# A fused attention and feed-forward kernel on one core: a step more in layer 2's feature chain, later outputs, new pacing of weights and rows

## The chip, the cores and the metric

The kernel runs on one core of one Trainium2 chip. The time is device microseconds of one launch; it was 992.25 us before the change (median of 3 runs, 991.57 to 992.88). The engines are TensorE (PE; its weight loads are PEld), VectorE (DVE), ScalarE (ACT), GpSimd (POOL) and SyncE (SP, which issues nearly all transfers). Each works through its own queue in order.

## The reference

```python
q_p, k_p = phi(q * scale), phi(k * scale)      # phi: exp(h - max h) / sqrt(m), h = x @ omega.T - |x|^2 / 2
kv, z = einsum('bhsm,bhsd->bhmd', k_p, v), sum(k_p, axis=2)
x = (q_p @ kv) / (q_p @ z + 1e-6)              # 4 batches, 8 heads, 576 rows, 64 columns; 128 features
x = x as 2304 x 512
# layer 1: d_ff 1536
xn = x / sqrt(mean(x * x) + 1e-6) * rms_g
x = (silu(xn @ w_gate) * (xn @ w_val)) @ w_out
# layer 2: d_ff 2048
h = x @ w_in
out = (h * cos(h)) @ w_out2                    # 2304 x 512
```

All inputs and the output are float32. The matrix products of the two layers are made of values split in a high and a low part, with three matmuls (high x high, low x high, high x low) in place of one.

## The kernel before

The 2304 tokens are cut in six blocks of 384, and these in three pairs. After attention, layer 1 runs over three groups of features; its second and third group (g = 1 and 2) and all of layer 2 use Strassen-like products: a pair of blocks and a pair of 128-feature tiles take seven products in place of eight. For these the rows of a pair are combined beforehand into T1 to T4 (`mix`, L1111, for layer 2; stored in DRAM and brought back by `bring`, L931).

Layer 2 is a sequence of 24 *periods* (`periods`, L1165): each has one pair of blocks (p) and one pair of feature tiles (fq). In the loop at L1349 a period k issues seven products with `hidden(k, i)`, L1176 (six matmuls of 384 columns each), and behind each product `share[i]` matmuls of the second product of an earlier period (`out2`, L1229, taken one at a time from `stream`; 36 a period, of 512 columns). Period 0's products are woven into the end of layer 1, and what is left of `out2` runs after the loop. Period 1 takes 26 output matmuls, all others 36; so the outputs are 10 matmuls behind a full period.

The products of a period alternate between two PSUM banks, X and Y. ScalarE copies the products 0, 2, 3 and 6 into SBUF (L1190), VectorE adds the others to these (L1193). The next product on a bank needs the copy or the addition before it.

A list of due work sets the order of everything else. `unit()` (L1012 shows in the profile for work issued by it) is called twice a product, so a period has 14 steps; `at(d, f)` puts f into the queues d steps later. A step also advances the preparation of weights by `tempo` (two rates, in parts of a step each).

`cosine` (L1204) turns two rows of h into features in this way: step 1 the phase as an integer (ScalarE), step 2 the two-part reduction (VectorE, L1214 and L1215), step 3 the sine (ScalarE), step 4 the multiplication by h (VectorE, L1225), steps 5 and 6 the split into high (ScalarE, L1046) and low (VectorE, L1049).

Weights come as chunks. A *front* (L187) undoes the packing of a raw chunk: VectorE at L190, L195 and L204, ScalarE at L182 for the next chunk, GpSimd at L209; it asks the raw chunk after next (L170), must wait until the next one's load was asked 9 steps ago (`LAG_OF_RAW`), and the result goes to DRAM (`kept`). A *back* brings chunks in again, combines and splits them (VectorE L274 to L291, ScalarE L214, GpSimd L217); it needs two fronts more than its own chunk, and room in a ring of 20 buffers, which `freed_by` (L1340) opens. Of 56 chunks beyond the first, `FRONTS_BY_2` wants 39 done before layer 2. Within it the rate of fronts is

```python
tempo[:] = 0.0 if loading or k < 4 else wts.rate(len(wts.todo) + 1, 14 * (14 - k)), 0.5 if loading else 1.3
```

where `loading` marks the last period of a run on one pair (k = 2, 5, 11, 14, 19, 21, 23), and `rate(chunks, steps)` spreads the fronts up to that chunk over so many steps.

In layer 1's groups 1 and 2, output rows y go to DRAM and are asked back (`ask`, L1091) some steps (`later`, L1302) after a product of the second half of a session, so that `add_y` (L1099) can add the next sums to them.

Of the kernel before, what the change touches and what calls it, by code (L numbers as in the profile page):

```python
# [38 lines left out]
AF = mybir.ActivationFunctionType  # L39
ALU = mybir.AluOpType  # L40
# [16 lines left out]
def attention_then_ffn(ctx: ExitStack, tc: tile.TileContext, qT, kT, v, omT, wc1, rms_g, wc2, out, B, H, S, D):  # L57
    nc = tc.nc
# [54 lines left out]
    def f32(ap):  # L113
        return ap.bitcast(F32)
# [3 lines left out]
    quarter = const.tile([P, 1], F32, name="quarter")  # L118
    half_pi = const.tile([P, 1], F32, name="half_pi")
# [7 lines left out]
    class Weights:  # L127
# [91 lines left out]
        def split(self, src, key):  # L219
            t = self.buffer()  # L220
            self.high(src, t, slice(0, 512))
            yield
            self.low(src, t, slice(0, 512))
            layer, f, e = key
            if self.paired(layer, f, e) == 0:
                self.out[layer, f, "A11"], self.out[layer, f, "A12"] = (t, 0), (t, 256)
            else:
                self.out[key] = t
            yield
# [172 lines left out]
    wts = Weights()  # L402
# [142 lines left out]
    with tc.manual_schedule():  # L545
# [59 lines left out]
        def job(n):  # L605
            for _ in range(n):
                if len(combined) < limit[0] and jobs and next(jobs[0][1], DONE) is DONE:
                    combined.add(jobs.pop(0)[0])
# [135 lines left out]
        for s, (nm, t) in tiles.items():  # L744
# [4 lines left out]
            else:  # L749
                for i in range(1, 8):  # L750
                    at = s + i + (s >= SLOTS - 1 or i > 1)
# [111 lines left out]
        def silu(blk, f, ps):  # L863
            a = row(F32, f"gv{blk}_{f}")
            nc.scalar.activation(a, ps, AF.Silu)
            return a
# [10 lines left out]
        def out1(g, blk, f, t, first, last, es):  # L877

            if first and es[0] == 0:
                yacc[blk] = [bank_of_sums(f"y_ps{g}_{blk}_{f}_{e}")[:, :NB] for e in range(KD)]  # L880
            w = wts.get(1, f, 2)
            for i, j in ((0, 0), (1, 0), (0, 1)):
                for e in es:
                    nc.tensor.matmul(yacc[blk][e], w[:, i, e * P:(e + 1) * P], t[:, j],  # L884
                                     start=first and i + j == 0, stop=last and j == 1)
            if not last:
                return
            for e in es:
                waits.append((put_away, blk, e, yacc[blk][e]))
# [26 lines left out]
        def halves(name):  # L916
            n = made["t"] % (OWN + EXTRA)
            made["t"] += 1
            if n < OWN:
                return fp.tile([P, 2, NB], F32R, tag="t", name=name, bufs=OWN)  # L920
            return more[0].tile([P, 2, NB], F32R, tag="t", name=name, bufs=EXTRA)

        def two_rows(dt, name):
            return more[0].tile([P, 2, NB], dt, tag="f", name=name, bufs=4)
# [23 lines left out]
        for n, (g, blk, f, first, last) in enumerate(steps):  # L948
# [13 lines left out]
            a = silu(blk, f, ps)  # L962
# [40 lines left out]
        tempo = [0.0, 0.0]  # L1003

        def at(d, f, *args):
            due.setdefault(clock[0] + d, []).append((f, args))

        def unit():
            now = due.setdefault(clock[0], [])
            while now:  # L1010
                f, args = now.pop(0)
                f(*args)  # L1012
            del due[clock[0]]
            flush(1)
            wts.now += 1
            wts.pace(*tempo)
            job(2 if clock[0] % 5 < 2 else 1)
            clock[0] += 1
# [147 lines left out]
        NPER = len(periods)  # L1166
        ends_run = [k + 1 == NPER or periods[k + 1][2] != periods[k][2] for k in range(NPER)]
        begins_run = [k == 0 or ends_run[k - 1] for k in range(NPER)]
# [35 lines left out]
        def cosine(k, h, of, begin=1):  # L1204

            name = "_".join(f"{x}_{f}_{blk}" for x, f, blk in of)
            span = slice(0, 2) if len(of) == 2 else slice(begin, begin + 1)
            h = h[:, span]
            a = two_rows(I32, f"turns{name}")[:, span]
            b = f32(halves(f"r{name}"))[:, span]  # L1210
            r = f32(a)

            def reduce():
                nc.vector.scalar_tensor_tensor(b, a, -TWO_PI_HI, h, op0=ALU.mult, op1=ALU.add)  # L1214
                nc.vector.scalar_tensor_tensor(r, a, -TWO_PI_LO, b, op0=ALU.mult, op1=ALU.add)  # L1215

            def cut(i):
                o = turned[of[i]] = halves("o%d_%d_%d" % of[i])
                split(o, r[:, i])
                at(int(of[i][0] + 1 < NPER), lower, o, r[:, i], nc.vector)  # L1220

            at(1, nc.scalar.activation, a, h, AF.Identity, quarter, 1.0 / (2 * math.pi))
            at(2, reduce)
            at(3, nc.scalar.activation, r, r, AF.Sin, half_pi)
            at(4, lambda: nc.vector.tensor_tensor(r, h, r, op=ALU.mult))  # L1225
            for i in range(len(of)):
                at(5 + i, cut, i)

        def out2(k):  # L1229

# [57 lines left out]
        for k, (g, p) in enumerate(pairs):  # L1288
            fs = list(GROUPS1[g])
            start = base + (g - 1) * PER_GROUP  # L1290
            last_of_group = k + 1 == len(pairs) or pairs[k + 1][0] != g
            nxt = pairs[k + 1] if k + 1 < len(pairs) else (3, sessions[0][1])
            left = UNITS * (len(pairs) - 1 - k) - (30 if k == 0 else 0)
            if k == NPAIR:
                while jobs:
                    job(1)
                combine.close()
                wider.append(extra.enter_context(tc.tile_pool(name="rows", bufs=1, reuse_waits="tile")))
                made["y"] = 0
            front[0] = wts.rate(FRONTS_BY_2, left) if left > 0 else 0.0  # L1300
            tt = {}
            later = 3 if g == 1 else 9  # L1302

            def after_first(i, f):
                if k == 0 and i == 0 and f == fs[1]:
                    out1(*steps[-1][:3], hid.pop(N1 - 1), *steps[-1][3:], range(KD))
                    wts.freed = C1 * G

            def after_second(i, f):
                if f == fs[3]:  # L1310
                    if nxt[0] == 3 or nxt[1] != p:
                        at(2, bring, *nxt, NAMES[i])
                    if i < KD:
                        at(later, ask, g, 2 * p, i)
                    elif i < 7:
                        at(later, ask, g, 2 * p + 1, i - KD)

            duo(g, p, fs[:2], w_bank, tt, after_first)
            if last_of_group:
                wts.freed = start + PER_PAIR  # L1320
            duo(g, p, fs[2:], bank_of_sums, tt, after_second)
            if last_of_group:
                wts.freed = start + 2 * PER_PAIR
            ys(g, p, 0, fs, tt, w_bank)
            at(6, ask, g, 2 * p + 1, 3)
            weave = None
            if k + 1 == len(pairs):
                weave = [lambda i=i: (hidden(0, i), unit()) for i in range(7)]
            ys(g, p, 1, fs, tt, bank_of_sums, weave)
            if last_of_group:  # L1330
                wts.freed = start + PER_GROUP
            if g == 2:
                for m, (name, kk) in enumerate((name, kk) for kk in range(2) for name in ("T1", "T3", "T2", "T4")):
                    at(6 + 3 * m // 2 if p else 6 + (0, 2, 3, 6)[m % 4] + 14 * kk, mix, p, name, kk)

        def stream():
            for k in range(NPER):
                yield from out2(k)

        def freed_by(k):  # L1340
# [4 lines left out]
            elif sessions[n - 1][0] != g and fq == GROUPS2[g][0]:  # L1345
                wts.freed = first_tile[g]

        o = stream()
        for k in range(1, NPER):  # L1349
            loading = ends_run[k]  # L1350
            tempo[:] = 0.0 if loading or k < 4 else wts.rate(len(wts.todo) + 1, 14 * (14 - k)), 0.5 if loading else 1.3
            if ends_run[k - 1]:
                ask_sums(k - 1)
            share = [2, 3, 3, 4, 4, 5, 5] if k == 1 else [5, 5, 3, 5, 6, 6, 6] if begins_run[k - 1] else [5, 5, 5, 5, 5, 5, 6]
            for i in range(7):
                if (k, i) == (len(GROUPS2[0]), 4):
                    assert not whole
                    wider.pop()
                    extra.close()
                    outs.append(ctx.enter_context(tc.tile_pool(name="outs", bufs=1, reuse_waits="tile")))  # L1360
                hidden(k, i)
                unit()
                for _ in range(share[i]):
                    next(o)
                unit()
                if i == 1 and k > 1:
                    freed_by(k - 1)
                if (i, k + 1) == (3, NPER):
                    ask_sums(k)
# [53 lines left out]
```

## Time and profile before

| what | value |
|---|---|
| median of 3 runs | 992.25 us |
| profiled execution | 990.3 us |
| its span | 988.5 us |
| TensorE busy | 957.0 us, 97% |
| VectorE busy | 730.0 us, 74% |
| ScalarE busy | 532.0 us, 54% |
| GpSimd busy | 412.1 us, 42% |
| granted TensorE clock | 0.998 of full |

Busy times are unions of instruction times of one profiled execution. Shares are means over stages that differ, so stretches are looked at by themselves below. In rows of the trace, an instruction's row has its start and duration in us, and in brackets how long its engine stood idle before it and what ended that.

### The profile page before, as it was taken

The numbers are of one execution on the slowest core, as the hardware profiler recorded it, in microseconds if no ns is written. First come the engines' busy times: TensorE is split into PE (matmuls) and PEld (weight loads), VectorE is DVE, ScalarE is ACT, GpSimd is POOL, SyncE is SP. The second block draws the span as 40 slices with busy tenths as digits, with TensorE's granted clock in tenths as the row PEclk, the third lists the DMA queues.
The fourth block names the chain that finished last, engine by engine and source line by source line (L and its number), as shares of the span: only waits on it lengthen the run. The fifth ranks groups of instructions, "written<-read, shape, count | busy, mean of one in ns | idle before, by whom it ended". The sixth has DMA issues, their size and how long they took to land.

```text
span 988.5 us, 16243 instructions
## 1 busy us (share of the span) xinstructions
PE 957.0 (97%) x5761; PEld 895.3 (91%) x5761; DVE 730.0 (74%) x1175; ACT 532.0 (54%) x1143; POOL 412.1 (42%) x377
## 2 busy tenths in 40 slices
PE   9999999998999999999999997999988999999998
PEld 8998999998999999999999996989867879898987
DVE  6787678898854785576786659887898897776766
ACT  7787676676434442535353636554554645464443
POOL 3143348648926875455664743211334121040000
PEclk9999999999999999999999999999999999999999
DMA  8555268876796988766979793857533848306564
GB/s 310 156 175 173 85 226 281 275 286 213 268 334 235 393 279 319 246 191 216 345 270 389 255 343 103 308 187 239 181 127 113 282 139 300 115 22 225 203 253 150
DMA packets 96082, 227.65 MB, mean 230 GB/s; under 512 B 9728, under 2 KB 45184, under 8 KB 96000
## 3 DMA queue, kind: packets, MB, share of 16 engines
q1 hardware_dynamic: 94560, 221.81, 64.8%
q10 hardware_dynamic: 1440, 4.78, 1.4%
q8 instruction: 46, 0.75, 0.3%
q14 instruction: 36, 0.29, 0.1%
HBM read 156.04 MB, written 70.52 MB: 229 GB/s over the span
## 4 chain that ended last, share of the span: by engine, by line
PE 61%; DVE 13%; DMA 8%; issue 6%; POOL 5%; ACT 5%; SPq 1%; ACTq 0%; DVEq 0%; POOLq 0%
PE o_ps L1242 14%; PE Xh L1038 7%; PE gv_ps L831 6%; PE X L1038 6%; PE Yh L1038 5%; PE Y L1038 4%; PE kv_ps L587 4%; PE y L1144 4%; PE y_ps L884 3%; DMA y<-y_dram 3%; PE num_ps L464 2%; PE kp_ps L426 2%; DMA T<-T_dram 1%; DVE r L1214 1%; PE qp_ps L426 1%
## 5 line engine op out<-in xcount | busy, mean ns | idle before, releaser
L1242 PE MATMUL o_ps<-w,o 128*128 128x512 f32 x864 | 225.7, 393 | 1.0 <-DVE o L1274 0.8
L209 POOL TENSOR_TENSOR f<-f,raw 128x512 f32<-128x512 f32 x68 | 94.5, 1390 | 225.2 <-DVE raw L204 193.3
L217 POOL TENSOR_TENSOR w<-b,w 128x512 fp32r<-128x512 f32 x88 | 116.1, 1325 | 169.7 <-ACT w L214 147.0
L1242 PEld LDWEIGHTS o_ps<-w,o 128*128 128x128 f32 x864 | 159.6, 188 | 25.7 <-DVE o L1274 1.1
L831 PE MATMUL gv_ps<-xhl,w 128*128 128x384 f32 x576 | 109.8, 339 | 1.5 <-DVE eT L454 1.3
L1144 PE MATMUL y<-t,w 128*128 128x384 f32 x576 | 102.7, 335 | 1.8 <-POOL w L217 1.8
L831 PEld LDWEIGHTS gv_ps<-xhl,w 128*128 128x128 f32 x576 | 101.8, 190 | 2.6 <-DVE eT L454 2.0
L1144 PEld LDWEIGHTS y<-t,w 128*128 128x128 f32 x576 | 99.9, 188 | 2.8 <-POOL w L217 2.8
L1038 PE MATMUL Xh<-T,w 128*128 128x384 f32 x432 | 88.9, 340 | 5.3 <-ACT h L1190 5.3
L1038 PEld LDWEIGHTS Xh<-T,w 128*128 128x128 f32 x432 | 77.8, 188 | 13.6 <-ACT h L1190 8.2
L1012 ACT ACTIVATE turns<-turns,half_pi 128x768 f32<-128x768 f32 (+1 forms) x50 | 45.6, 913 | 76.7 <-DVE turns L1215 76.7
L1038 PE MATMUL X<-T,w 128*128 128x384 f32 x432 | 81.1, 335 | 0.5 <-POOL w L217 0.3
L1038 PEld LDWEIGHTS X<-T,w 128*128 128x128 f32 x432 | 75.3, 188 | 1.1 <-POOL w L217 0.7
L1012 ACT ACTIVATE turns<-h,quarter 128x768 int32<-128x768 f32 (+1 forms) x50 | 45.6, 912 | 56.6 <-DVE h L1193 56.5
L1225 DVE TENSOR_TENSOR turns<-h,turns 128x768 f32<-128x768 f32 (+1 forms) x50 | 50.6, 1012 | 31.3 <-ACT turns L1012 31.1
L214 ACT CAST w<-b 128x512 fp32r<-128x512 f32 x88 | 50.7, 581 | 30.7 <-DVE b L274 28.2
L1049 DVE TENSOR_TENSOR o<-turns,o 128x384 fp32r<-128x384 f32 x96 | 64.8, 704 | 2.5 <-ACT o L1046 1.3
L1038 PE MATMUL Yh<-B,w 128*128 128x384 f32 x288 | 59.3, 340 | 7.1 <-ACT h L1190 5.7
L1214 DVE SCALAR_TENSOR_TENSOR r<-turns,h 128x768 f32<-128x768 int32 (+1 forms) x50 | 50.2, 1004 | 21.2 <-ACT turns L1012 20.8
L1038 PEld LDWEIGHTS Yh<-B,w 128*128 128x128 f32 x288 | 51.7, 188 | 13.0 <-ACT h L1190 8.0
L884 PE MATMUL y_ps<-t,w 128*128 128x384 f32 x288 | 60.7, 346 | 0.0
L1046 ACT CAST o<-turns 128x384 fp32r<-128x384 f32 x96 | 45.8, 512 | 25.5 <-DVE turns L1225 24.4
(118 smaller groups left out, 1863.9 us busy)
## 6 DMA issues: line engine op xcount, KB each, us to landing
T<-T_dram SPq DMA_DIRECT2D x48, 768.0 KB, 7.0
raw<-wc SPq DMA_DIRECT2D x59, 512.0 KB, 5.0
B<-yh_dram SPq DMA_DIRECT2D x21, 768.0 KB, 5.3
kept<-f SPq DMA_DIRECT2D x56, 256.0 KB, 5.1
b<-kept SPq DMA_DIRECT2D x56, 256.0 KB, 4.6
B<-x_dram SPq DMA_DIRECT2D x15, 768.0 KB, 6.4
x_dram<-xhl SPq DMA_DIRECT2D x12, 768.0 KB, 5.8
s<-x_dram SPq DMA_DIRECT2D x24, 384.0 KB, 6.1
```

What stands on the lines that cost most here:

```text
L209: nc.gpsimd.tensor_tensor(f32(f), f32(f), rest, op=ALU.add)
L214: nc.scalar.copy(t[:, 0, to], src)
L217: nc.gpsimd.tensor_tensor(t[:, 1, to], src, f32(t[:, 0, to]), op=ALU.subtract)
L831: nc.tensor.matmul(o, w[i], x[j], start=n == 0, stop=n == len(terms) - 1)
L884: nc.tensor.matmul(yacc[blk][e], w[:, i, e * P:(e + 1) * P], t[:, j], start=first and i + j == 0, stop=last and j == 1)
L1012: f(*args)
L1038: nc.tensor.matmul(o, w[:, i, c + kk * P:c + (kk + 1) * P], x[:, j, kk], start=begin and n == 0, stop=n == 5, skip_group_check=True)
L1049: engine.tensor_tensor(t[:, 1], a, f32(t[:, 0]), op=ALU.subtract)
L1144: nc.tensor.matmul(acc[e], w[:, i, e * P:(e + 1) * P], t[:, j], start=f == fs[0] and i + j == 0, stop=f == fs[-1] and j == 1)
L1214: nc.vector.scalar_tensor_tensor(b, a, -TWO_PI_HI, h, op0=ALU.mult, op1=ALU.add)
L1225: at(4, lambda: nc.vector.tensor_tensor(r, h, r, op=ALU.mult))
L1242: nc.tensor.matmul(oacc[blk][j], o[:, x, js], w[:, y], start=first and n == 0, stop=last and n == 2)
```

## The change

The chain in `cosine` gets one step more between phase and reduction and one more between reduction and sine, in all periods but the last. Period 1 issues 21 output matmuls in place of 26, so outputs are 15 behind. Rooms in the ring of weights are opened at product 2 in place of product 1. The rate of fronts follows a table of goals per period. The asks of y rows in group 2 come 7 steps after their product in place of 9, and the eight combinations of the pairs 2 and 1 are spread over 8 steps in place of 10.

```diff
@@ cosine
-            at(1, nc.scalar.activation, a, h, AF.Identity, quarter, 1.0 / (2 * math.pi))
-            at(2, reduce)
-            at(3, nc.scalar.activation, r, r, AF.Sin, half_pi)
-            at(4, lambda: nc.vector.tensor_tensor(r, h, r, op=ALU.mult))
+            ph, re, si, mu, cu = (1, 2, 3, 4, 5) if k + 1 == NPER else (1, 3, 5, 6, 7)
+            at(ph, nc.scalar.activation, a, h, AF.Identity, quarter, 1.0 / (2 * math.pi))
+            at(re, reduce)
+            at(si, nc.scalar.activation, r, r, AF.Sin, half_pi)
+            at(mu, lambda: nc.vector.tensor_tensor(r, h, r, op=ALU.mult))
             for i in range(len(of)):
-                at(5 + i, cut, i)
+                at(cu + i, cut, i)
@@ layer 1, groups 1 and 2
-            later = 3 if g == 1 else 9
+            later = 3 if g == 1 else 7
...
-                    at(6 + 3 * m // 2 if p else 6 + (0, 2, 3, 6)[m % 4] + 14 * kk, mix, p, name, kk)
+                    at(6 + 5 * m // 4 if p else 6 + (0, 2, 3, 6)[m % 4] + 14 * kk, mix, p, name, kk)
@@ layer 2
+        FRONT_GOALS = {3: 42, 4: 45, 6: 47, 7: 48, 8: 49, 9: 50, 12: 52, 13: 54, 15: 56, 16: 57}
...
-            tempo[:] = 0.0 if loading or k < 4 else wts.rate(len(wts.todo) + 1, 14 * (14 - k)), 0.5 if loading else 1.3
+            tempo[:] = wts.rate(wts.fused + FRONT_GOALS[k], 14) if k in FRONT_GOALS else 0.0, 0.5 if loading else 1.3
...
-            share = [2, 3, 3, 4, 4, 5, 5] if k == 1 else [5, 5, 3, 5, 6, 6, 6] if begins_run[k - 1] else [5, 5, 5, 5, 5, 5, 6]
+            share = [1, 2, 3, 3, 4, 4, 4] if k == 1 else [5, 5, 3, 5, 6, 6, 6] if begins_run[k - 1] else [5, 5, 5, 5, 5, 5, 6]
...
-                if i == 1 and k > 1:
+                if i == 2 and k > 1:
                     freed_by(k - 1)
```

## Rows read from the trace of the kernel before

**Rows 1.** Busy time by stretch: periods k = 1, 2, 3, 4, 8, 9, 10, 11, 13, 16.
```profile
core 0: us, PE busy (x) PEld busy (x) DVE busy (x) ACT busy (x) POOL busy (x), PEclk, DMA share, GB/s
...
593.43:610.58 17.15, 14.43 (x69) 11.66 (x68) 15.50 (x27) 11.10 (x22) 5.28 (x3) 1.00 0.21 77
610.58:628.92 18.34, 16.11 (x80) 14.20 (x80) 17.67 (x24) 10.58 (x20) 6.84 (x7) 1.00 0.80 287
628.92:644.67 15.75, 15.75 (x79) 14.19 (x78) 12.75 (x16) 7.08 (x12) 3.95 (x3) 1.00 0.56 221
644.67:660.39 15.72, 15.72 (x79) 14.15 (x78) 13.51 (x23) 9.39 (x16) 1.31 (x1) 1.00 0.57 200
...
707.62:725.99 18.37, 16.45 (x79) 13.84 (x77) 16.20 (x20) 9.26 (x18) 7.26 (x5) 1.00 0.39 127
725.99:746.08 20.09, 16.54 (x79) 13.93 (x79) 18.62 (x23) 10.01 (x19) 8.98 (x7) 1.00 0.42 128
746.08:765.96 19.88, 16.80 (x79) 13.84 (x79) 17.11 (x24) 10.49 (x19) 8.90 (x7) 1.00 0.38 111
765.96:782.30 16.34, 16.11 (x79) 14.20 (x80) 13.29 (x16) 10.00 (x17) 4.46 (x4) 1.00 0.87 302
...
798.05:816.84 18.79, 16.62 (x80) 13.89 (x79) 17.91 (x30) 10.22 (x18) 6.04 (x4) 1.00 0.41 140
...
848.34:864.06 15.72, 15.72 (x79) 14.15 (x78) 13.29 (x20) 7.73 (x14) 1.14 (x1) 1.00 0.51 168
```

**Rows 2.** TensorE's instructions in order of time, four that it had to wait for.
```profile
512.96 2.35 PE L1038 MATMUL Y<-T,w 128*128 128x384 f32 x12 [1.54 <-DVE r L1069]
...
581.79 1.31 PE L1038 MATMUL Yh<-B,w 128*128 128x384 f32 x6 [1.43 <-DVE y L1099]
...
740.62 1.31 PE L1038 MATMUL Yh<-B,w 128*128 128x384 f32 x6 [2.43 <-ACT h L1190]
...
804.52 0.98 PE L1242 MATMUL o_ps<-w,o 128*128 128x512 f32 x3 [0.82 <-DVE o L1274]
```

**Rows 3.** ScalarE's instructions in order of time, ahead of the stall at 740.62.
```profile
739.27 0.94 ACT L1012 ACTIVATE turns<-turns,half_pi 128x768 f32<-128x768 f32 x1 [3.21 <-DVE turns L1215]
740.11 0.46 ACT L1190 COPY h<-Yh 128x384 f32<-128x384 f32 x1
```

**Rows 4.** Who waited for whom, whole run: total us, times, longest.
```profile
ACT turns L1012 <- DVE turns L1215: 76.7, 49, 3.9
```

**Rows 5.** VectorE's instructions in order of time, of the first product and of k = 9.
```profile
581.17 0.56 DVE L1099 TENSOR_TENSOR y<-y,y 128x384 f32<-128x384 f32 x1 [1.82 <-DMA y<-y_dram]
...
727.01 1.30 DVE L1214 SCALAR_TENSOR_TENSOR r<-turns,h 128x768 f32<-128x768 int32 x1 [0.74 <-ACT turns L1012]
...
736.20 2.04 DVE L1214 SCALAR_TENSOR_TENSOR r<-turns,h 128x768 f32<-128x768 int32 x1
...
740.23 0.96 DVE L1225 TENSOR_TENSOR turns<-h,turns 128x768 f32<-128x768 f32 x1 [0.66 <-ACT turns L1012]
...
745.14 0.41 DVE L190 TENSOR_SCALAR f<-W 128x512 int32<-128x512 int32 x1
```

**Rows 6.** GpSimd's instructions in order of time, beside L1214 at 736.20.
```profile
736.13 1.29 POOL L217 TENSOR_TENSOR w<-b,w 128x512 fp32r<-128x512 f32 x1 [0.27 <-ACT w L214]
```

**Rows 7.** Groups by line, 630 to 990 us: count, busy us, mean ns, idle before.
```profile
L1242 PE MATMUL o_ps<-w,o 128*128 128x512 f32 x802 | 209.1, 393 | 1.0 <-DVE o L1274 0.8
...
L209 POOL TENSOR_TENSOR f<-f,raw 128x512 f32<-128x512 f32 x17 | 23.7, 1392 | 95.2 <-DVE raw L204 65.6 <-issue 13.1 <-PE Yh L1038 9.1
...
L204 DVE SCALAR_TENSOR_TENSOR raw<-raw 128x512 f32<-128x512 uint32 x17 | 11.6, 685 | 0.0
...
L195 DVE TENSOR_SCALAR raw<-f 128x512 int32<-128x512 int32 x17 | 8.4, 493 | 0.0
```

**Rows 8.** Busy time of L209 alone by stretch: k = 3, 4, 10, 13.
```profile
628.92:644.67 15.75, 0.00 (x0) 1.00 0.56 221
644.67:660.39 15.72, 1.31 (x1) 1.00 0.57 200
...
746.08:765.96 19.88, 3.00 (x2) 1.00 0.38 111
...
798.05:816.84 18.79, 4.59 (x3) 1.00 0.41 140
```

## The prediction

> **What bounds the kernel now.** I read the page's slices first: TensorE is close to full throughout. No edit of the diff adds or removes a matmul, so the change can only take away, add or move the time in which TensorE stands still. Next I cut layer 2 into its 24 periods (k = 0 to 23, from the first product of one to the first of the next) and asked for the busy times of each [rows 1]. A period without a stall takes 15.75 us (k = 3, 4, 16). The long ones are k = 8, 9, 10, 11 and 13, with 18.37, 20.09, 19.88, 16.34 and 18.79 us: together 14.7 us over 15.75. Earlier, k = 2 is 2.6 over, and k = 1 takes 17.15 us although it holds ten matmuls fewer. From k = 14 on the periods are like k = 16. In the four longest VectorE is busy for 16.2 to 18.6 us: more than the 15.75 that TensorE needs.
>
> Third, the matmuls in order of time say on whom TensorE waits: at 740.62 it stood for 2.43 us until ScalarE had copied a product out of PSUM (L1190) [rows 2]. ScalarE was not busy then. Its queue stood at the sine for 3.21 us waiting for VectorE's reduction, and the copy came right behind [rows 3]; over the whole run ScalarE waits 76.7 us at its sines in this way, 49 times [rows 4]. VectorE in turn was late because its first reduction (L1214) took 2.04 us beside a GpSimd instruction that began at 736.13 and took 1.29 [rows 5, 6], while an operation of the same size elsewhere takes 0.96; and because it had itself waited 0.74 us for the phase and 0.66 us for the sine at the heads of its queue [rows 5]. So the chain is: too much on VectorE, lengthened by GpSimd; the sine late; the copy behind it late; TensorE idle.
>
> **The change part by part.**
>
> *Fronts to other periods.* One front (conversion of a weight chunk) costs VectorE three operations, 0.41 (L190, free) [rows 5], 0.49 (L195) and 0.69 (L204) [rows 7], and its GpSimd add can hold a VectorE operation by up to 2.04 - 0.96 = 1.08 us; bounds 0 and 1.08, taken at the middle, 0.55, since some adds meet no such operation. That makes 2.1 us (1.6 to 2.7). By the adds per period [rows 8], of the 17 fronts after k = 2 [rows 7] none are done in k = 3, one in k = 4, two in each of k = 6 to 10 (the row of k = 10 stands for five alike), three in k = 13. The new goals allow 3 each in k = 3 and 4, then 2, 1, 1, 1 in k = 6 to 9, none in 10, 2 each in 12, 13, 15 and 1 in 16. But a front must wait until a chunk's raw load is 9 steps old (LAG_OF_RAW), so I expect only two adds to get through in each of k = 3 and 4, and the remainder in k = 6 and 7. Against before: k = 3 +2, k = 4 +1, k = 8 -1, k = 9 -1, k = 10 -2, k = 13 -1, k = 16 +1.
>
> VectorE's busy time then becomes, from rows 1: k = 8 14.1, k = 9 16.5, k = 10 12.9, k = 11 13.3, k = 13 15.8; on the other side k = 3 17.0, k = 4 15.6, k = 16 15.4.
>
> SyncE gets the fronts' raw loads and stores with them; no new bytes. The backs need a chunk two fronts ahead: 39 are done at the end of layer 1, at least 43 by the end of k = 4, and k = 9 wants 37 to 40, so no weight becomes late.
>
> *The chain one step wider.* The reduction now comes two steps (of about 15.75/14 = 1.13 us) behind the phase, and the sine two behind the reduction. The two reductions take twice 0.96, longer than one step, which is why the sine waited. VectorE's wait for the phase (0.74) goes; that for the sine stays, since the multiplication is still one step behind it. Of 1.47 us idle of VectorE in k = 9 I keep 0.8 (bounds 0 and 1.5). A period then takes the larger of 15.75 and busy + 0.8: k = 3 17.8, k = 4 16.4, k = 9 17.3, k = 13 16.6, k = 16 16.2, the others 15.75. Stalls left: 2.0 + 0.7 + 1.5 + 0.9 + 0.5 = 5.6 us in place of 14.7. Gain 9.1 us.
>
> The extra life of the buffers costs nothing: the rows of h and turns are reused a period (14 steps) later, and the chain now uses them for 6 steps in place of 4; the halves' ring of 8 has at least 4 steps to spare. Chain and outputs move by two steps together, so a feature is still ready some 5 steps before its first matmul. Were that cover gone, the wait would be TensorE's, at most the two steps.
>
> *Outputs 15 matmuls behind.* They are the same matmuls. In k = 1 five fewer of them cover the waits for VectorE (15.50 busy of 17.15 [rows 1]); 802 of them take 209.1 us [rows 7], 0.26 each, so between 0 and 1.3 us is lost, taken as 0.6. k = 2 stays as it is: its VectorE has 17.67 us of work, and neither front nor mix of the last pair moves. At a run's end the third bank of the first block now has one product fewer between its last old and first new matmul. One wait of 0.82 us of this kind is there, at 804.52, in a crowded period [rows 2]; six run ends bound it at 4.9, and I take 0 because the other five show none. Weights are released two steps later; the store of an eviction, and the loads of kept weights, go on SyncE's queue as much later. In the tail five more matmuls stand behind the last sine; the last period's chain is unchanged and it already ends without a stall: 0.
>
> *y rows.* The asks of group 2 come two steps earlier, about 2.1 us at six matmuls a step. The one stall that they reach is 1.43 us at 581.79, behind an addition (L1099) that waited 1.82 us for its row's transfer [rows 2, 5]. Bounds 0 and 1.4; taken 1.0 gained. They pass transfers of layer 2's first operands on SyncE's queue, which have some microseconds before their products.
>
> *Mix.* Pairs 2 and 1 do their eight combinations in 8 steps in place of 10. The subtractions and their GpSimd parts stand closer, the stores on SyncE go earlier and free rows sooner for the earlier asks. The stall of 1.54 us at 512.96, behind VectorE (L1069) [rows 2], lies in such a stretch; it could go or double: -1.5 to +1.5, taken 0.
>
> **Sum.** 9.1 - 0.6 + 1.0 = 9.5 us. The profiled execution took 990.3 us (span 988.5 and 1.8 around it), the median of the runs is 992.25; 9.5 off gives 980.8 and 982.75. I predict the latter.
>
> **A rule of the Trainium skill** weighed against the row: its page "SBUF — State Buffer", section "Who interferes with whom", says that a VectorE instruction with two SBUF inputs and a GpSimd instruction that reads SBUF lock each other out for the whole instruction. The 2.04 beside 0.96 agrees in kind. If every front's add held VectorE for its whole time (1.39 us mean [rows 7]), a front would cost 3.0, the stalls left would be about 7 us (k = 3 and 4 worse, k = 9 and 13 better), and the gain some 1.5 less.
>
> **Rivals.**
>
> *Early overload (slower).* VectorE is already the bound in k = 1 and 2, and the change puts work right behind them. If all three fronts get through in each of k = 3 and 4 at 2.7 us, and VectorE keeps its 1.5 us of waits, k = 3 takes 12.75 + 8.1 + 1.5 = 22.4 and k = 4 13.51 + 5.4 + 1.5 = 20.4: 11.2 us lost, 12.4 with k = 1. The later periods then give back 14.7 less (1.5 + 0.9 + 0.5 + 3 x 0.7) = 9.7. Net +2.7: 995 us. It decides from about five fronts in k = 3 and 4. For it: VectorE's 17.67 in k = 2. Against: the 9 steps of lag.
>
> *Everything clears.* The wider chain is the real cure, ScalarE no longer stands at the sine, and k = 2 and 3 lose nothing either: 14.7 + 2.6 + 1.4 (the y stall) - 0.6 = 18.1 us: 974. For it: TensorE waits mostly on the copy behind the sine. Against: k = 2 has more VectorE work than matmul time, whatever the order.
>
> *Only the fronts help, the chain does not.* VectorE's idle time stays 1.5 and evictions wait at some run ends: 9.5 less 3.5 (five periods, 0.7 each) and less 2 (a few of the 0.82): about 988.
>
> *The goals do little.* Fronts slip to where they were, stalls are only moved: 991 to 993. Against: tempo is zero in k = 10 and 11, so two fronts surely leave k = 10.
>
> **How the numbers follow.** Forecast 0.60 (own range 977 to 987), everything clears 0.10, only fronts 0.10, no change 0.08, early overload 0.12. A measurement of this kernel tells about 0.2% (2 us): faster 0.80, same 0.08, slower 0.12. The range takes in all but the far end of the two outer cases: 975.5 to 991.
>
> **What would show it.** In the changed trace: no TensorE wait over 1 us in k = 8, 10 and 11; one short one in k = 9; VectorE near 17 us in k = 3, with new stalls there of about 2 us; the sine's wait on VectorE (L1215) well under its 76.7 us [rows 4], the reduction's wait on ScalarE near zero; the y stall under 0.5. Wrong would be: four or more us lost in k = 3 and 4, or stalls of k = 9 and 13 as long as now.

## The result, and the profile after

The changed kernel takes 977.11 us (median of 4 runs, 976.38 to 978.14); the kernel before, beside it, 991.91. The ratio is 0.985, 95% interval 0.9833 to 0.9867: 14.8 us faster. That lies in the range (975.5 to 991) and has the forecast sign, but it is more than half as much again as the 9.5 us forecast, at the very edge of the forecast's own range (977 to 987). The profiled execution took 976.7 us, its span 974.9; before 990.3 and 988.5.

First the same view as [rows 1], busy time by stretch, of the changed kernel: periods k = 1, 2, 3, 4, 8, 9, 10, 11, 13 and 16. The first number behind the stretch is its length, then PE, PEld, DVE, ACT and POOL.

```profile
core 0: us, PE busy (x) PEld busy (x) DVE busy (x) ACT busy (x) POOL busy (x), PEclk, DMA share, GB/s
...
590.45:605.27 14.82, 12.94 (x64) 10.95 (x63) 14.75 (x24) 9.29 (x19) 5.24 (x3) 1.00 0.20 72
605.27:623.53 18.26, 16.61 (x79) 14.00 (x79) 17.73 (x23) 11.77 (x22) 6.85 (x6) 1.00 0.73 261
623.53:640.00 16.47, 16.00 (x80) 14.09 (x78) 16.01 (x23) 7.57 (x13) 5.95 (x4) 1.00 0.93 353
640.00:658.59 18.59, 16.26 (x79) 13.99 (x78) 18.27 (x30) 11.11 (x21) 5.36 (x4) 1.00 0.50 171
...
705.82:721.57 15.75, 15.75 (x79) 14.20 (x78) 12.74 (x16) 9.30 (x17) 6.62 (x5) 1.00 0.27 89
721.57:737.32 15.75, 15.75 (x79) 14.04 (x78) 14.90 (x18) 8.19 (x17) 8.38 (x6) 1.00 0.32 101
737.32:753.16 15.84, 15.84 (x79) 14.28 (x79) 14.42 (x20) 10.89 (x20) 6.25 (x5) 1.00 0.05 17
753.16:768.92 15.76, 15.76 (x80) 14.19 (x78) 13.12 (x16) 7.99 (x14) 5.26 (x3) 1.00 0.82 267
...
784.67:800.39 15.72, 15.72 (x79) 14.15 (x78) 13.47 (x22) 9.12 (x17) 4.97 (x4) 1.00 0.62 203
...
831.90:848.47 16.57, 16.00 (x80) 14.12 (x79) 14.09 (x21) 7.52 (x13) 3.40 (x3) 1.00 0.48 174
```

k = 8 to 13 are clean: the 14.7 us above 15.75 of before are 0.1. k = 3 and 4, clean before, now lose 3.6 us, k = 16 loses 0.8. k = 1 is 2.3 us shorter, of which its five matmuls less are 1.2 to 1.3; k = 2 is as it was. Not shown here: the first product of layer 2 starts at 576.93 in place of 578.11, period 0 takes 13.52 us in place of 15.33, k = 21 is 0.3 us longer, and the stretch behind the last period's first product is 1.7 us longer, 1.2 of them the five delayed matmuls. These pieces add up to the 13.6 us between the two spans. Of the 1.2 us at the first product of layer 2, 0.6 are already there at the first product of layer 1 (300.96 in place of 301.59), which no part of the change reaches: they belong to these two executions and not to the change.

TensorE's instructions in order of time, the rows with a wait in brackets, answer to [rows 2]:

```profile
600.59 0.73 PE L1243 MATMUL o_ps<-w,o 128*128 128x512 f32 x2 [1.16 <-DVE o L1049]
...
613.78 1.31 PE L1038 MATMUL Yh<-T,w 128*128 128x384 f32 x6 [1.25 <-DVE h L1193]
...
647.47 1.33 PE L1038 MATMUL Yh<-T,w 128*128 128x384 f32 x6 [1.13 <-DVE h L1193]
...
650.47 0.96 PE L1243 MATMUL o_ps<-w,o 128*128 128x512 f32 x3 [1.20 <-DVE o L1275]
```

These are four of the six waits over 0.5 us left between 570 and 860 us: two in the crowded k = 1 and 2, two in k = 4 (one for an addition, one for an eviction at the end of a run). The other two are of 0.72 us in k = 1 and of 0.57 in k = 16. The wait at the first product is gone.

Who waited for whom in the whole run, against [rows 4]; first further rows of before, then the changed kernel:

```profile
DVE turns L1225 <- ACT turns L1012: 31.1, 41, 1.0
...
ACT o L1046 <- DVE turns L1225: 24.4, 33, 1.6
...
DVE r L1214 <- ACT turns L1012: 20.8, 23, 1.1
```

```profile
ACT o L1046 <- DVE turns L1226: 81.6, 47, 2.6
...
ACT turns L1012 <- DVE turns L1215: 33.0, 33, 2.9
...
DVE r L1214 <- ACT turns L1012: 4.1, 12, 1.1
...
DVE turns L1226 <- ACT turns L1012: 1.7, 4, 0.7
```

ScalarE's wait at the sine fell from 76.7 to 33.0 us, VectorE's wait for the phase from 20.8 to 4.1 and its wait for the sine, at the multiplication, from 31.1 to 1.7. ScalarE's idle time in all falls only by about as much as the span (span less busy: 974.9 - 531.0 = 443.9 us, before 456.5), for it now waits 81.6 us for the multiplication, ahead of the split (24.4 before). What has changed is what stands behind its waits. One period shows how; k = 9 in order of time, ScalarE first, then VectorE, then GpSimd:

```profile
730.64 0.48 ACT L1190 COPY h<-Yh 128x384 f32<-128x384 f32 x1
733.39 0.94 ACT L1012 ACTIVATE turns<-turns,half_pi 128x768 f32<-128x768 f32 x1 [2.27 <-DVE turns L1215]
```

```profile
731.42 1.94 DVE L1215 SCALAR_TENSOR_TENSOR turns<-turns,r 128x768 f32<-128x768 int32 x1
```

```profile
730.82 1.72 POOL L217 TENSOR_TENSOR w<-b,w 128x512 fp32r<-128x512 f32 x1 [0.58 <-ACT w L214]
```

A reduction still takes double its time beside a GpSimd instruction (1.94 in place of 0.96) and the sine still waits 2.27 us. But the copy of the product (L1190 at 730.64) now stands in front of the sine in ScalarE's queue, not behind it as in [rows 3].

### The profile page after: what moved, and what is told of

The parts are those of the page before. It is cut to its first block, busy times and chain, and to the rows that moved or that the text cites. A ratio compares the mean times of both kernels' runs of the same rounds, so it can differ in the third digit from the quotient of the medians.

```text
span 974.9 us, 16229 instructions
## 1 busy us (share of the span) xinstructions
PE 954.4 (98%) x5761; PEld 895.4 (92%) x5761; DVE 729.1 (75%) x1175; ACT 531.0 (54%) x1143; POOL 418.1 (43%) x377
## 5 line engine op out<-in xcount | busy, mean ns | idle before, releaser
L209 POOL TENSOR_TENSOR f<-f,raw 128x512 f32<-128x512 f32 x68 | 96.0, 1411 | 239.7 <-DVE raw L204 168.7
L217 POOL TENSOR_TENSOR w<-b,w 128x512 fp32r<-128x512 f32 x88 | 118.9, 1359 | 126.9 <-ACT w L214 117.2
L1046 ACT CAST o<-turns 128x384 fp32r<-128x384 f32 x96 | 47.2, 513 | 81.6 <-DVE turns L1226 81.6
L1049 DVE TENSOR_TENSOR o<-turns,o 128x384 fp32r<-128x384 f32 x96 | 61.7, 659 | 8.5 <-ACT o L1046 8.1
L204 DVE SCALAR_TENSOR_TENSOR raw<-raw 128x512 f32<-128x512 uint32 x68 | 57.0, 838 | 0.6
L1215 DVE SCALAR_TENSOR_TENSOR turns<-turns,r 128x768 f32<-128x768 int32 (+1 forms) x50 | 54.3, 1087 | 1.7
L1193 DVE TENSOR_TENSOR h<-Yh,h 128x384 f32<-128x384 f32 x48 | 26.5, 553 | 38.6 <-PE Yh L1038 38.6
```

The source lines that it names most:

```text
L204: nc.vector.scalar_tensor_tensor(rest, raw[:, :, 0].bitcast(U32), 2.0 ** -52, rest, op0=ALU.mult, op1=ALU.mult)
L209: nc.gpsimd.tensor_tensor(f32(f), f32(f), rest, op=ALU.add)
L217: nc.gpsimd.tensor_tensor(t[:, 1, to], src, f32(t[:, 0, to]), op=ALU.subtract)
L1046: nc.scalar.copy(t[:, 0], a)
L1049: engine.tensor_tensor(t[:, 1], a, f32(t[:, 0]), op=ALU.subtract)
```

## The experiments

All are measured beside the kernel before, on one chip for each group: the first four, the next four, the next three, the last one. "Lost" is the sum over 15.75 us a period in the profiled execution.

| kernel | median, us | ratio to before (95%) | lost in k = 8 to 13 | in k = 3 and 4 |
|---|---|---|---|---|
| before | 991.9 | 1 | 14.7 | 0 |
| all of the change | 977.11 | 0.985 (0.9833 to 0.9867) | 0.1 | 3.6 |
| chain and delay | 984.09 | 0.9926 (0.9909 to 0.9944) | 7.0 | 0 |
| goals alone | 988.06 | 0.9968 (0.9955 to 0.9981) | 4.3 | 3.2 |
| rows and mix alone | 987.20 | 0.9956 (0.9939 to 0.9972) | 14.7 | 0 |
| chain alone | 982.20 | 0.9902 (0.9886 to 0.9919) | 7.4 | 0 |
| delay alone | 998.37 | 1.0058 (1.0036 to 1.008) | 18.1 | 0.6 |
| all but the goals | 980.63 | 0.9892 (0.9876 to 0.9908) | 7.0 | 0 |
| before, adds left out | 985.96 | 0.9941 (0.9929 to 0.9954) | 7.8 | 0 |
| all, goals later | 977.97 | 0.9859 (0.9846 to 0.9871) | 1.5 | 1.7 |
| all but the delay | 979.58 | 0.9888 (0.9873 to 0.9904) | 0.4 | 3.8 |
| reduction later | 987.49 | 0.9964 (0.9952 to 0.9977) | 9.6 | 0.2 |
| sine later | 985.81 | 0.995 (0.9938 to 0.9963) | 8.2 | 0 |
| all, goals also in k = 5 | 976.98 | 0.9845 (0.9828 to 0.9862) | 0 | 2.6 |

**Chain and delay.** Before, with these lines of the change:

```diff
+            ph, re, si, mu, cu = (1, 2, 3, 4, 5) if k + 1 == NPER else (1, 3, 5, 6, 7)
+            share = [1, 2, 3, 3, 4, 4, 4] if k == 1 else ...
+                if i == 2 and k > 1:
```

> Before, with the wider chain, outputs 15 behind and rooms opened at product 2; fronts, rows and mix as before. Theory F (the fronts' VectorE work in k = 8 to 13 made the stalls): only the queues' idle time goes, about 0.7 us in each of five periods, so 2 to 5 us faster, with 8 us or more of stalls left in k = 8 to 13. Rival Q (the sine and the reduction at the heads of the queues made them): 10 to 14 us faster, and k = 8 to 13 nearly clean although two fronts a period are still done there.

7.3 us faster by the ratio: between the two. Half of the loss in k = 8 to 13 goes with the fronts where they were, and 7.0 us stay. Neither theory holds alone.

**Goals alone.**

```diff
+            tempo[:] = wts.rate(wts.fused + FRONT_GOALS[k], 14) if k in FRONT_GOALS else 0.0, ...
```

> Before, with the table of goals alone. Theory F: k = 8 to 13 lose 5 us or less in place of 14.7, k = 3 and 4 lose 3 to 5: 5 to 8 us faster. Rival Q: the sine still holds the copies, k = 9 and 10 keep more than half of their stall, k = 3 and 4 lose as much as is won: within 3 us of before.

3.2 us faster: under theory F's 5 to 8, just over the rival's 3, with the losses about where F put them (4.3 and 3.2). What is missing is elsewhere: period 0 takes 17.59 us (before 15.33), k = 2 takes 19.87 (before 18.33), and k = 9 takes 20.05 although VectorE has less to do. This profile is of the slowest of the twelve runs (990.32 us), so it shows more loss than the median run has. The stretch rows of k = 9 and 10 of this kernel show what happens there (PEclk is the third number from the end):

```profile
732.21:752.26 20.05, 17.81 (x80) 15.30 (x79) 16.59 (x21) 10.61 (x20) 7.65 (x6) 0.91 0.33 93
752.26:768.01 15.75, 15.75 (x79) 14.19 (x78) 12.05 (x18) 9.46 (x17) 6.42 (x5) 1.00 0.00 0
```

The clock granted to TensorE was 0.91 of full in k = 9, and TensorE is busy for 17.81 us with matmuls that take 15.75 in k = 10. The clock fell after this wait of TensorE, of 2.08 us (its instructions in order of time):

```profile
745.95 1.31 PE L1038 MATMUL Yh<-B,w 128*128 128x384 f32 x6 [2.08 <-ACT h L1190]
```

**Rows and mix alone.**

```diff
+            later = 3 if g == 1 else 7
+                    at(6 + 5 * m // 4 if p else ...
```

> Before, with the asks of y two steps earlier and the closer mix alone. If these gave the 1.2 us by which period 0 starts earlier and the 1.8 by which it is shorter: 2 to 3 us faster, and no stall at the first product of layer 2. If the y stall went for another reason (later loads of kept weights, another order of transfers): 0 to 1 us.

4.4 us faster, more than either. Period 0 takes 13.52 us, as in every kernel here that has this part, while it takes 15.1 to 17.6 in those that have not. The row comes in time: the addition that before waited 1.82 us at 581.17 [rows 5] waits less, and no product stands behind it (VectorE in order of time).

```profile
579.89 0.56 DVE L1099 TENSOR_TENSOR y<-y,y 128x384 f32<-128x384 f32 x1 [1.37 <-DMA y<-y_dram]
```

In layer 1 the wait of 1.54 us at 512.96 [rows 2] is 1.11 here, and from layer 1's first combined product to period 0 the kernel takes 275.6 us in place of 276.5. The two edits of this part were not tried one by one.

**Chain alone.** The first line of the first experiment without the other two.

> Before, with the wider chain alone, outputs still 10 behind. The features then come two steps later at outputs that do not move: by the steps there are 3 left of 5, so the chain's whole gain should be here too, the same time as with the later outputs within 1.5 us. If the 5 matmuls of delay are needed as cover, TensorE waits at the outputs (on VectorE's low part) in many periods, and the time is 3 us or more above the run with both.

9.7 us faster, and 2.4 more than with the delay, though the two intervals overlap: the wider chain is the largest part of the change by itself. TensorE does wait at the outputs for the split of their features (L1046 on ScalarE, L1049 on VectorE), but only in k = 1 (its instructions in order of time):

```profile
602.02 0.74 PE L1243 MATMUL o_ps<-w,o 128*128 128x512 f32 x2 [1.11 <-ACT o L1046]
...
604.58 0.50 PE L1243 MATMUL o_ps<-w,o 128*128 128x512 f32 x1 [1.82 <-DVE o L1049]
```

The busy times by stretch of k = 8, 9, 10 and 13 show what stays:

```profile
707.37:723.12 15.75, 15.75 (x79) 14.20 (x78) 14.15 (x18) 8.42 (x16) 7.85 (x6) 1.00 0.40 120
723.12:741.26 18.14, 16.48 (x80) 13.74 (x78) 18.07 (x22) 9.91 (x18) 10.34 (x7) 1.00 0.45 140
741.26:759.61 18.35, 16.74 (x79) 13.94 (x79) 17.18 (x24) 10.60 (x19) 8.46 (x6) 1.00 0.39 106
...
791.22:809.29 18.07, 16.34 (x80) 13.95 (x79) 17.35 (x27) 9.50 (x17) 4.59 (x4) 1.00 0.44 157
```

In k = 9 VectorE is busy for 18.07 of 18.14 us. Before it was 18.62 of 20.09 [rows 1]: its idle 1.47 us are gone. In k = 10 and 13 it still stands idle for 1.17 and 0.72. What is left in all three is more VectorE time than the 15.75 us of the matmuls, its holds beside GpSimd counted as busy; fewer fronts take it away, as the whole change shows.

**Delay alone.** The other two lines, which were not tried one by one.

> Before, with outputs 15 behind and rooms opened at product 2 alone. By the prediction's step: 0 to 1.3 us slower, from less cover in k = 1, nothing at the run ends. If the delay by itself helps (a run's first outputs and the evictions stand better), 1 to 3 us faster, seen in k = 8 to 13.

5.8 us slower, worse than both. k = 13, in which the outputs of one run end and those of the next begin, takes 22.18 us (the stretch, then TensorE's instructions in order of time):

```profile
803.36:825.54 22.18, 19.12 (x79) 16.14 (x78) 19.53 (x32) 10.33 (x19) 5.54 (x4) 0.85 0.37 131
```

```profile
813.73 1.02 PE L1242 MATMUL o_ps<-w,o 128*128 128x512 f32 x3 [2.37 <-DVE o L1274]
...
817.37 2.93 PE L1242 MATMUL o_ps<-w,o 128*128 128x512 f32 x6 [0.69 <-ACT o L1276]
```

The outputs of the next run wait for evictions of the last; of these waits before had one, of 0.82 us [rows 2]. Then the clock falls (0.85 in the period). The six runs of this kernel lie far apart, from 993.51 us at a mean clock of 0.997 to 1000.61 at 0.991, so a part of the 5.8 us is the clock: from the mean clocks (0.9935 over its runs, 0.9962 over those of before beside it) I estimate at most 2.7.

**All but the goals.** The changed kernel with the old rate of fronts.

> The changed kernel with the old rate of fronts. Theory F: 6 to 9 us slower than the changed kernel, stalls back in k = 9, 10 and 13, none in k = 3 and 4. Rival Q: k = 8 to 13 stay clean, k = 3 and 4 lose nothing: as fast or 2 to 3 us faster than the changed kernel.

The ratio is 0.0042 above that of the whole change: about 4 us, under theory F's 6 to 9. The 7.0 us in k = 8 to 13 are back, k = 3 and 4 are clean.

**Adds left out.** Before, without GpSimd's add in the fronts of layer 2.

```diff
-            nc.gpsimd.tensor_tensor(f32(f), f32(f), rest, op=ALU.add)
+            if c < self.fused + 39:
+                nc.gpsimd.tensor_tensor(f32(f), f32(f), rest, op=ALU.add)
```

> Before, with GpSimd's adds at the end of a front left out for the 17 chunks done in layer 2 (the low part of these weights is then missing; VectorE's and ScalarE's share of the fronts stays). It shows the price of the shared port. At 0.55 us for each add, as predicted, k = 8 to 13 win about 6 us of their 14.7. At the whole 1.3 us each: 12 or more. At nothing: 0, and the fronts' cost is VectorE's own 1.6 us alone.

7.0 us won in k = 8 to 13, where 11 of the adds are done: 0.63 us of TensorE's time for each. What an add holds VectorE is more: VectorE's busy time in the whole run, 730.0 us before, is 714.9 here, 0.89 us less for each of the 17 adds. The prediction took 0.55, in bounds of 0 and 1.08. The busy times of this kernel's page:

```profile
PE 957.6 (97%) x5761; PEld 898.0 (91%) x5761; DVE 714.9 (73%) x1175; ACT 532.8 (54%) x1143; POOL 389.6 (40%) x360
```

In all it is 5.9 us faster. The waits that stay are the old ones (lines are one further down here):

```profile
737.48 1.31 PE L1039 MATMUL Yh<-B,w 128*128 128x384 f32 x6 [1.02 <-ACT h L1191]
...
806.75 1.31 PE L1039 MATMUL Yh<-B,w 128*128 128x384 f32 x6 [1.51 <-ACT h L1191]
```

**Goals later.** `{3: 41, 4: 42, 6: 45, 7: 47, 8: 48, 9: 50, ...}`.

> The changed kernel with goals 41 and 42 in k = 3 and 4, 45 in 6, 47 in 7, 48 in 8: two fronts moved out of k = 3 and 4. If VectorE's load of 18.3 us in k = 4 is what its 2.8 us stall comes from, the stall of k = 4 falls under 1, k = 6 and 7 (11.7 and 15.6 us of VectorE) stay under 16, and the time is 2 to 3 us below the changed kernel. If it comes from the eviction at the run's end, the stall stays and the time is the same.

A miss: the same time. k = 4 falls from 18.59 to 17.24 us, but k = 7, 9 and 10 lose 2.5 us; the work is only moved.

**All but the delay.**

> The changed kernel with outputs 10 behind again and rooms opened at product 1 (chain, goals, rows and mix stay). The wider chain without the delay was 1.9 us faster than with it. If the delay costs that in any company: about 975, 1 to 3 us below the changed kernel, the wait for evictions near 841 us and the 0.8 us of k = 16 gone. If the delay pays only together with the goals: slower than the changed kernel.

The expected gain did not come: the ratio is 0.0038 worse than the whole change's. By itself, and with the chain, the delay costs; with all the rest it pays. k = 2 is clean (15.78), the 0.8 us of k = 16 are gone, but k = 1 takes 19.51 us and k = 7 17.50 (the stretch of k = 1, a part of it, and then TensorE's instructions):

```profile
591.30:610.81 19.51, 16.58 (x70) 14.48 (x70) 18.16 (x27) 12.29 (x24) 6.61 (x5) 0.83 0.28 94
600.40:607.20 6.80, 5.76 (x16) 5.28 (x17) 5.87 (x11) 2.61 (x5) 2.29 (x2) 0.50 0.48 156
```

```profile
598.89 0.73 PE L1243 MATMUL o_ps<-w,o 128*128 128x512 f32 x2 [1.12 <-ACT o L1046]
...
601.44 0.80 PE L1243 MATMUL o_ps<-w,o 128*128 128x512 f32 x1 [1.82 <-DVE o L1049]
...
702.32 1.45 PE L1243 MATMUL o_ps<-w,o 128*128 128x512 f32 x5 [1.49 <-ACT o L1277]
```

In k = 1 TensorE runs out of outputs whose features are ready, twice. From 600.40 to 607.20, from within the second of these waits on, it runs at 0.50 of its clock. All four runs of this kernel show a mean clock of 0.994 to 0.996, those of the changed kernel 0.998 to 1.000. Over a span of 976 us the means of the two (0.9945 and 0.9985) are 3.9 us apart, which is an estimate of the most that the clock can cost here: it is as much as the whole gain of the delay.

**Reduction later, sine later.** Before, with one of the two gaps: steps (1, 3, 4, 5, 6) and (1, 2, 4, 5, 6).

> Before, with the reduction two steps behind the phase, all later steps of the chain one later (sine still one step behind the reduction). It takes away VectorE's wait for the phase (20.8 us in the run), and leaves ScalarE's wait for the reduction (76.7). If VectorE's time is what counts: most of the wider chain's 9.5 us, 6 to 9 faster. If the copies behind the sine count: 0 to 3 us faster.

> Before, with the sine two steps behind the reduction, the later steps one later (reduction still one step behind the phase). It takes away most of ScalarE's wait of 76.7 us at the sine and leaves VectorE's 20.8 us for the phase. If the copies behind the sine are what TensorE waits for: 6 to 9 us faster. If VectorE's time counts: 0 to 3 us faster.

3.6 and 5.0 us faster by the ratios; together 8.6, and the wider chain has 9.7. Neither expectation of a single queue holds: each gap gives about its share. Their waits in the whole run, first with the reduction later, then with the sine later:

```profile
ACT turns L1012 <- DVE turns L1215: 44.0, 29, 3.4
...
DVE r L1214 <- ACT turns L1012: 8.9, 22, 0.6
```

```profile
ACT turns L1012 <- DVE turns L1215: 26.2, 25, 2.6
...
DVE r L1214 <- ACT turns L1012: 19.3, 33, 1.5
```

**Goals also in k = 5.** `{3: 41, 4: 43, 5: 45, 6: 47, ...}`.

> The changed kernel with goals 41, 43 and 45 in k = 3, 4 and 5 (before 42, 45 and none): the fronts of k = 4 are spread into k = 5, whose VectorE is busy for 12 of 15.8 us. If k = 4's 2.8 us of stall are VectorE's load there (18.3 us): k = 4 falls to about 16 to 17 us and k = 5 stays clean, 1.5 to 2.5 us below the changed kernel's 977. If the transfers that begin a run (operands loaded in k = 5) or the evictions set it: the same time, or slower.

The same time again (0.9845 against 0.985). VectorE's work in k = 4 falls by 1.1 us, the loss by 0.4; TensorE waits there for evictions (the stretch, then TensorE's instructions):

```profile
641.37:659.56 18.19, 16.27 (x80) 14.02 (x79) 17.15 (x28) 10.60 (x20) 4.57 (x3) 1.00 0.53 180
```

```profile
650.60 0.96 PE L1243 MATMUL o_ps<-w,o 128*128 128x512 f32 x3 [1.36 <-DVE o L1275]
...
655.60 1.66 PE L1243 MATMUL o_ps<-w,o 128*128 128x512 f32 x6 [0.56 <-DVE o L1275]
```

So the rival of that expectation is the better one: in k = 4 the ends of a run count beside the load (with the goals later, where VectorE's load in k = 4 was 16.07 us in place of 18.27, the period was 1.35 shorter). No kernel here is clearly faster than the changed one.

## Why the prediction was right, and where it was too small

**The bound** was read rightly: the time was lost in k = 8 to 13 to VectorE's load and to waits at the heads of two queues, and chain and goals clear it together (14.7 us to 0.1, and to 0.4 without the delay), neither alone (7.4 and 4.3 left). "Only the fronts help, the chain does not" is refuted: alone the chain gives 9.7, the goals 3.2. The prediction put both into one sum and so did not see that the chain alone gives more than the goals alone. Left out of the whole change, the goals cost about 4 us; the chain was not left out of it by itself.

**The chain's term was too small.** I kept 0.8 us of VectorE's idle time in a period because its wait for the sine would stay, so that k = 9 and 13 would lose 2.4 us more. That wait did not stay: 31.1 us before, 1.7 after. In the changed kernel k = 7 has 15.55 us of VectorE work in 15.72 and no stall:

```profile
690.10:705.82 15.72, 15.72 (x80) 14.15 (x78) 15.55 (x24) 9.39 (x17) 4.52 (x4) 1.00 0.76 262
```

But the larger slip for k = 9 and 13 is VectorE's work itself: I worked out 16.5 and 15.8 us, and it is 14.90 and 13.47. At these even the kept 0.8 would have cost nothing.

**The fronts.** Two adds each were foreseen in k = 3 and 4; the changed kernel has one in k = 3 and three in k = 4 (four in all, as foreseen). The price of 2.1 us was low, within its range of 1.6 to 2.7: the add's hold on VectorE measured 0.89, taken 0.55. Beside the kernel with all but the goals, the changed one has six adds less in k = 8 to 13 (5 in place of 11) and 14.0 us less of VectorE's busy time there (79.6 in place of 93.6): 2.3 us a front. The page "SBUF — State Buffer" of the Trainium skill, section "Who interferes with whom", has the loser wait for the whole instruction. The 1.94 us reduction above agrees for the one that is hit; as a mean over adds VectorE loses 0.89 of 1.39 us. The loss in k = 3 and 4, 2.7 foreseen, is 3.6: VectorE's 18.27 us in k = 4, with its third add, stand against 15.6 worked out.

**The y rows and the mix** were taken at 1.0 and measured 4.4 alone. I priced one stall of one execution. Period 0 takes 15.1 to 17.6 us (mean 16.4) in the eight kernels without this part and 13.52 in all with it; the profile of before, with 15.33, was one of the better cases. Of what else this part gives, 0.9 us lie in layer 1, where I had taken the mix at 0.

**The delay** was priced at 0.6 lost. Alone it loses 5.8, beside the chain 2.4, and in the whole change it wins 3.8 (0.985 against 0.9888). I reasoned from VectorE's cover in k = 1 and took the run ends as free; both were wrong in size (k = 16 and 21, in which a run's outputs end, lose 0.8 and 0.3 in the kernels that have chain and delay). Why it pays only in the whole change is not shown. In the traces it moves the stall between k = 1 and k = 2: beside the chain k = 1 takes 14.84 us in place of 18.46 and k = 2 18.27 in place of 15.78; in the whole change it spares 4.7 us in k = 1, five matmuls and a fall of the clock among them, and 1.8 in k = 7, and costs 2.5 in k = 2. That a fall of the clock follows such waits was in no step of mine. How much of the 3.8 us is the clock stays open; the 6.8 us at half of it in the one trace are worth at most 3.4, the mean clocks of all runs at most 3.9.

**The clock** can be a part of the 14.8 us as well. The 46 runs of before that stand beside the experiments have a mean clock of 0.9965, the four of the changed kernel 0.9985: that is worth at most 2 us, by estimate. The two profiled executions both had 0.998, and their spans are 13.6 us apart.

**The rivals.** Early overload did not come: k = 3 and 4 lose 3.6, not 11. "Everything clears" (974) came nearer to the measured time than the forecast: k = 8 to 13 did clear, k = 2 did not (18.26), as its VectorE load said.

## What to carry to other kernels

Where one engine's queue holds a short copy that TensorE needs behind an operation that waits for another engine, move the waiting operation further from its producer: here one step more at two places was worth 9.7 us with the same work done. Then move work out of the stretches in which the engine is full, not on average but period by period, and expect each fix to leave the other's loss visible. Measure the parts of a schedule change in company as well as alone: the delay cost 5.8 us alone and was worth 3.8 beside the rest. And read the granted clock of every run before a difference is put down to the schedule: here up to 2.7 of those 5.8 us, and perhaps all of the 3.8, are the clock.

## What was not expected of the hardware

TensorE's granted clock falls to half for some microseconds in the middle of a stretch in which it is nearly always busy. In the rows above the fall comes after a wait of 2.08 us (goals alone, k = 9), after one of 2.37 (delay alone, k = 13) and within one of 1.82 that followed one of 1.12 (all but the delay, k = 1: 0.50 from 600.40 to 607.20). That is 1.2 GHz in place of 2.4. In layer 2 the fourteen traces hold twelve such falls, in eight kernels; each begins in a wait of TensorE of 1.8 to 3.0 us, or less than 1.5 us behind one. Not each such wait is followed by one: before waited 2.43 us at 740.62 [rows 2] and that execution's k = 9 and 10 show 1.00 [rows 1]. The changed kernel's trace, in which the longest wait of layer 2 is 1.25 us, holds none. The page "TensorE: Matmul & The Clock Gate" of the Trainium skill, Part 1, lets the clock follow how busy the array has been; the rows agree in kind. So a stall can cost more than its length: with the goals alone k = 9 lost 4.3 us, a wait of 2.08 and 2.06 of slower matmuls among them.
